# One decode-attention kernel: heads gathered in one PSUM bank per side, normalized once, and wo rows sent whole through four column groups

## The chip, the cores and the metric

One Trainium2 chip, of which the kernel uses one core. The metric is the device time of one execution in microseconds (us); where several runs are shown, their median. Times inside an execution are counted from the start of its profiled span.

## What is computed

Two attention layers of one token, A and B, each with 32 heads of 128, a K and a V cache of 16,384 positions, and bf16 data. A reads its whole caches, B only the last 4,096 positions. Both results, 512 numbers each, are written side by side.

```python
# A (B the same, with k and v cut to their last W = 4096 positions)
q = (x @ wq).reshape(B, Sq, Hq, Dh)                 # x: 1 x 512, wq: 512 x 4096
scores = einsum("bhqd,bhkd->bhqk", q, k) * (Dh ** -0.5)
p = softmax(scores)
o = einsum("bhqk,bhkd->bhqd", p, v)
out_A = o.reshape(B, Sq, Hq * Dh) @ wo              # wo: 4096 x 512
out = concatenate([out_A, out_B], axis=-1)          # 1 x 1 x 1024
```

## The kernel before

**Tiles.** The work is cut into 20 tiles of 8 MB of K and 8 MB of V. A tile of side A holds two heads (`a_pair`): a head's positions lie on 64 partitions, 256 on each. A tile of side B holds two units of four heads (`b_window`), each head on 32 partitions with 128 positions on each. `steps` puts B's four tiles at places 0, 7, 13 and 19, so the last tile is one of B's, with two units.

**Scores on VectorE.** For each half of a tile, `scores_prod` (L202) multiplies K in place with q, spread over the partitions; `scores_tree` (L208, L212) adds the 128 products pairwise and reduces the last eight. `tile_max` (L220, L224) and `max_all` (L230, L234, L237) find the maximum of each head, by a transpose on TensorE, and bring it back to one number per partition; L237 is an f32 matmul with an identity.

**Softmax and V.** `soft` on ScalarE takes the exponentials with their sums per partition (L251, sums in `un.cs`) and multiplies them by a mask for each head (L258), so that one matmul serves all heads of a unit. `soft_sum` (L266) adds the sums of a head's partitions on TensorE, `recip` (L274) inverts them on VectorE. `pv` (L283) runs 64 (A) or 32 (one unit of B) matmuls of 512 columns: four positions at once, into four groups of PSUM rows (column groups of 32), which TensorE works on at the same time. Each head then has 4 x 4 partial results, in a bank of 128 x 512. L290 copies the bank out with the factor 1/sum, four f32 matmuls (L294) with slices of `fold` pick and add the right pieces, and L299 writes the heads' columns into `s.O` (128 x 32).

**The output projection.** `permute_o` (L303 to L312) turns `s.O` into the order in which wo's rows lie on the partitions (row 32p + r on partition p, `load_wo`), giving `s.Op`. `project_out` (L319) sends each of the 32 rows r through four column groups, 128 output columns to each: 128 matmuls of 128 columns per side, all 32 weight columns being copies of one column of `s.Op`. L329 or L332 casts, and one DMA per side stores four partitions of 128 numbers.

**Order and buffers.** The order is the one of the source (`manual_schedule`). Each engine works through its own instructions in that order; all loads are issued by SyncE (SP), x and A's store by ScalarE. K has two slots (`kring`), V one (`vring`); wo takes V's slot after the last but one `pv`, and the last V goes into a K slot. In step T, VectorE does tile T's scores, while the softmax and `pv` of tile T-1 run on the other engines. wo of A comes as one load of 4 MB, that of B in pieces of 16, 8, 4, 3 and 1 rows. After the last tile: `permute_o(A)`, maxima, softmax, sums, two `pv`, `permute_o(B)`, projections of A and of B.

The names that the prediction uses: `sm` (PSUM tile of maxima and sums), `o` (PSUM banks of `pv`), `oc`, `oT`, `op`, `OA`/`OB`, `OpA`/`OpB`, `out_rows`, `wot` (wo in memory), `vlast` (the last V).

Of the kernel before, what the change touches and what calls it, by code (L numbers as in the profile page):

```python
# [25 lines left out]
def kernel(  # L26
# [30 lines left out]
    ps_s = ctx.enter_context(tc.tile_pool(name="ps_s", bufs=2, space=bass.MemoryType.PSUM))  # L57
# [13 lines left out]
    ident = singles.tile([P, P], BF16, tag="ident")  # L71
    one_b = singles.tile([1, 1], BF16, tag="one_b")
    pick = singles.tile([HQ, P + 4], BF16, tag="pick")
    fold = singles.tile([P, QR], F32, tag="fold")

    A, B = _Side(), _Side()
    for k, (s, n, x, wq, wo, nh) in enumerate(((A, "A", A_x, A_wq, A_wo, 2), (B, "B", B_x, B_wq, B_wo, 4))):
        s.n, s.k, s.x, s.wq, s.wo, s.nh = n, k, x, wq, wo, nh
        s.units = 1 if s is A else 2
        s.xT = singles.tile([P, KC], BF16, tag=f"xT{n}", name=f"xT{n}")  # L80
        s.q = singles.tile([P, HQ // nh, DH], BF16, tag=f"q{n}", name=f"q{n}")
        s.O = singles.tile([P, HQ], BF16, tag=f"O{n}", name=f"O{n}")
        s.Op = singles.tile([P, HQ], BF16, tag=f"Op{n}", name=f"Op{n}")
        s.mask = singles.tile([P, nh], F32, tag=f"mask{n}", name=f"mask{n}")
        s.rows = singles.tile([P, P], F32, tag=f"rows{n}", name=f"rows{n}")
# [59 lines left out]
    def make_masks(s):  # L145
        nc.vector.tensor_reduce(out=s.mask[:, :], in_=by_head(s, identf[:, :]), axis=AX.X, op=ALU.add)
        G = P // (4 * s.nh)
        nc.vector.tensor_copy(
            s.rows[:, :].rearrange("p (g h c) -> p g h c", g=G, h=s.nh),
            s.mask[:, :].unsqueeze(1).unsqueeze(3).broadcast_to([P, G, s.nh, 4]),  # L150
        )

    def turn_x(s, xrow):
        ps = ps_t.tile([P, KC], F32, tag="tp", name="xps")
        xr = xrow[:, s.k, :].rearrange("o (p c) -> o c p", c=KC)
        for c in range(KC):
            nc.tensor.matmul(ps[:, c : c + 1], lhsT=xr[:, c, :], rhs=one_b[:, :], start=True, stop=True)
        nc.vector.tensor_copy(s.xT[:, :], ps[:, :])
# [57 lines left out]
    def tile_max(T):  # L216
        un = tiles[T]
        U = un.s.units
        m = small.tile([P, 2], F32, tag="m", name="m")
        nc.vector.tensor_reduce(  # L220
            out=m[:, 0:U], in_=un.sc[:, :].rearrange("p (u n) -> p u n", u=U), axis=AX.X, op=ALU.max
        )
        un.sm = ps_m.tile([P, 512], F32, tag="sm", name="sm")
        nc.tensor.transpose(un.sm[0:U, 0:P], m[:, 0:U], identf[:, :])  # L224

    def max_all(T):
        un = tiles[T]
        s, U = un.s, un.s.units
        M = small.tile([2, 4], F32, tag="M", name="M")
        nc.vector.tensor_reduce(  # L230
            out=M[0:U, 0 : s.nh], in_=by_head(s, un.sm[0:U, 0:P]), axis=AX.X, op=ALU.max
        )
        Mr = one.tile([2, P], F32, tag="Mr", name="Mr")
        nc.vector.tensor_copy(  # L234
            by_head(s, Mr[0:U, :]), M[0:U, 0 : s.nh].unsqueeze(2).broadcast_to([U, s.nh, P // s.nh])
        )
        nc.tensor.matmul(  # L237
            un.sm[:, 128 : 128 + U], lhsT=Mr[0:U, :], rhs=identf[0:U, 0:U], start=True, stop=True
        )

    def soft(T):
        un = tiles[T]
        s, U = un.s, un.s.units
        bias = small.tile([P, 2], F32, tag="bias", name="bias")
        nc.scalar.activation(out=bias[:, 0:U], in_=un.sm[:, 128 : 128 + U], func=ACT.Copy, scale=-inv)  # L245
        p = one.tile([P, 2 * CH], BF16, tag="p", name="p")
        un.cs = small.tile([P, 2], F32, tag="cs", name="cs")
        pm = one.tile([P, 8 * CH], BF16, tag="pm", name="pm")
        un.pm = []
        for u in range(U):  # L250
            nc.scalar.activation(  # L251
                out=un.part(p, u), in_=un.part(un.sc, u), func=ACT.Exp, scale=inv, bias=bias[:, u : u + 1],
                accum_out=un.cs[:, u : u + 1],
            )
            n = un.n * s.nh
            un.pm.append(pm[:, u * n : (u + 1) * n].rearrange("p (i h c) -> p i h c", h=s.nh, c=4))
            for j in range(s.nh):
                nc.scalar.activation(  # L258
                    out=un.pm[u][:, :, j, :], in_=un.part(p, u).rearrange("p (i c) -> p i c", c=4),
                    func=ACT.Copy, scale=s.mask[:, j : j + 1],  # L260
                )

    def soft_sum(T):
        un = tiles[T]
        U = un.s.units
        nc.tensor.matmul(  # L266
            un.sm[:, 136 : 136 + U], lhsT=un.s.rows[:, :], rhs=un.cs[:, 0:U], start=True, stop=True
        )

    def recip(T):  # L270
        un = tiles[T]
        U = un.s.units
        un.r = small.tile([P, 2], F32, tag="r", name="r")
        nc.vector.reciprocal(un.r[:, 0:U], un.sm[:, 136 : 136 + U])  # L274

    def pv(T, u):
# [13 lines left out]
        nc.scalar.activation(out=osb[:, :], in_=o[:, :], func=ACT.Copy, scale=un.r[:, u : u + 1])  # L290
        oc = ps_s.tile([P, 4], F32, tag="sp", name="oc")
        sel = fold[:, 0:rows].rearrange("k (h c) -> k c h", c=4)
        for j in range(4):
            nc.tensor.matmul(  # L294
                oc[:, 0 : s.nh], lhsT=osb[:, j * P : (j + 1) * P], rhs=sel[:, j, :],
                start=(j == 0), stop=(j == 3),
            )
        col = s.nh * (s.units * un.g + u)
        nc.scalar.copy(s.O[:, col : col + s.nh], oc[:, 0 : s.nh])  # L299

    def permute_o(s):
        oT = ps_t.tile([HQ, P], BF16, tag="tp", name="oT")
        nc.tensor.transpose(oT[:, :], s.O[:, :], ident[:, :])  # L303
        oTs = one.tile([HQ, P], BF16, tag="oTs", name="oTs")
        nc.scalar.copy(oTs[:, :], oT[:, :])
        op = ps_t.tile([P, HQ], F32, tag="tp", name="op")
        for j in range(4):
            nc.tensor.matmul(
                op[:, :], lhsT=pick[:, 4 - j : 4 - j + P], rhs=oTs[:, j * HQ : (j + 1) * HQ],
                start=(j == 0), stop=(j == 3),  # L310
            )
        nc.scalar.copy(s.Op[:, :], op[:, :])  # L312

    def project_out(s):
        w = DN // NG
        ps = ps_s.tile([P, w], F32, tag="sp", name="out_rows")
        for r in range(HQ):
            for g in range(NG):
                nc.tensor.matmul(  # L319
                    ps[QR * g : QR * (g + 1), :],  # L320
                    lhsT=s.Op[:, r : r + 1].broadcast_to([P, QR]),
                    rhs=s.wo_t[:, r, g * w : (g + 1) * w],
                    start=(r == 0), stop=(r == HQ - 1),
                )
        rows = one.tile([P, w], BF16, tag=f"rows_out{s.n}", name="rows_out")
        dst = out[0, 0, s.k * DN : (s.k + 1) * DN].rearrange("(g f) -> g f", g=NG)
        src = rows[:, :].rearrange("(g x) f -> g x f", g=NG)[:, 0, :]
        if s is A:
            nc.scalar.copy(rows[:, :], ps[:, :])  # L329
            nc.scalar.dma_start(out=dst, in_=src)  # L330
        else:
            nc.vector.tensor_copy(rows[:, :], ps[:, :])  # L332
            nc.sync.dma_start(out=dst, in_=src)

    wo_pieces = (16, 8, 4, 3, 1)
    with tc.manual_schedule():
        xrow = one.tile([1, 2, D], BF16, tag="pm", name="xrow")
        for s in (B, A):
            nc.scalar.dma_start(out=xrow[:, s.k, :], in_=s.x[0, :, :])
# [10 lines left out]
        nc.vector.memset(one_b[:, :], 1.0)  # L350
        nc.vector.tensor_copy(ident[:, :], identf[:, :])
        clear_x(B, flat(scratch[:, :, :]))
        clear_x(A, one.tile([P, 2 * KC * P], BF16, tag="o4", name="xbA")[:, :])
        zeros = flat(scratch[:, :, :])[:, 0 : 512]
        for o in o_banks:
            nc.tensor.matmul(o[:, :], lhsT=zeros[:, 0:P], rhs=zeros, start=True, stop=True)
        for s in (B, A):
            make_masks(s)
        nc.vector.tensor_reduce(
            out=fold[:, :], in_=identf[:, :].rearrange("p (g x) -> p x g", g=NG), axis=AX.X, op=ALU.add  # L360
        )
        nc.vector.memset(pick[:, :], 0.0)
        nc.vector.tensor_copy(
            pick[:, 4 : 4 + P].rearrange("h (m k) -> h m k", k=4)[:, :, 0], identf[0:HQ, 0:HQ]
        )
        for s in (B, A):
            turn_x(s, xrow)
# [5 lines left out]
        for T in range(NT):  # L373
# [7 lines left out]
            if T >= 1:  # L381
                max_all(T - 1)
                soft(T - 1)
                soft_sum(T - 1)
            scores_tree(T, 0)
            if T >= 1:
                recip(T - 1)
# [13 lines left out]
        permute_o(A)  # L401
        max_all(NT - 1)
        soft(NT - 1)
        soft_sum(NT - 1)
        recip(NT - 1)
        for u in range(2):
            pv(NT - 1, u)
        permute_o(B)
        project_out(A)
        project_out(B)  # L410
# [30 lines left out]
```

## Time and profile before

| | us |
|---|---|
| time, median of 3 runs (826.05 to 826.29) | 826.10 |
| time of the profiled execution | 825.77 |
| its span in the profile | 824.0 |
| VectorE (DVE) busy | 760.8 (92%) |
| TensorE matmuls (PE) busy | 203.3 (25%) |
| ScalarE (ACT) busy | 67.6 (8%) |
| mean granted TensorE clock | 0.584 of full |
| read from HBM | 352.32 MB, 428 GB/s over the span |

A group of the profile reads: line, engine, operation, tile written <- tiles read, shapes, count, then busy us and mean ns of one instruction, then the engine's idle time ahead of them and what ended it. PE is a matmul, PEld a weight load, SPq and ACTq are the parts of an engine that issue DMAs. An f32 matmul that is no transpose shows as two records. In the chain of waits "issue" is time for which the profile names no cause. The granted clock is the share of TensorE's full clock in a stretch; it takes the values 0.5 and 1.0, and other values are means.

### The profile page before, as it was taken

How to read it: one execution, taken by the hardware profiler on the slowest of the kernel's cores; microseconds unless marked ns; L12 is line 12 of the kernel's file. 1: busy time of each engine (PE TensorE's matmuls, PEld its weight loads, DVE VectorE, ACT ScalarE, POOL GpSimd, SP SyncE). 2: the span in 40 equal slices, each digit the busy share in tenths (PEclk: the TensorE clock that was granted, in tenths of full speed). 3: DMA queues.
4: the chain of work that ended last, by engine and by line, in shares of the span. 5: the costliest groups of instructions: out<-in, count | busy, mean ns of one | idle time of the engine just before them, and what ended most of it. 6: DMA issues, size and time to landing. Idle time of an engine off the chain costs nothing.

```text
span 824.0 us, 4577 instructions
## 1 busy us (share of the span) xinstructions
PE 203.3 (25%) x1912; PEld 101.1 (12%) x1912; DVE 760.8 (92%) x340; ACT 67.6 (8%) x192; POOL 0.7 (0%) x6
## 2 busy tenths in 40 slices
PE   4402212303030203230312213030503030303126
PEld 1101100101010101120101101010201010101014
DVE  2899999999999999999999999999999999999980
ACT  0102000001010000100000000010200000000011
POOL 0000000000000000000000000000000000000000
PEclk9765555565565655555655565555555565555567
DMA  9999999999999999999999999999999999999996
GB/s 383 434 439 427 452 433 431 439 426 437 426 439 429 421 442 443 414 452 423 440 426 440 426 439 416 447 426 423 440 442 424 445 427 439 424 425 441 421 433 282
DMA packets 8104, 352.61 MB, mean 428 GB/s; under 512 B 914, under 2 KB 1044, under 8 KB 1300
## 3 DMA queue, kind: packets, MB, share of 16 engines
q1 hardware_dynamic: 8072, 352.33, 99.1%
q8 instruction: 14, 0.23, 0.1%
q14 instruction: 6, 0.05, 0.0%
q10 hardware_dynamic: 12, 0.00, 0.0%
HBM read 352.32 MB, written 0.00 MB: 428 GB/s over the span
## 4 chain that ended last, share of the span: by engine, by line
DMA 48%; DVE 48%; PE 2%; issue 1%; ACT 1%; SPq 0%; DVEq 0%; ACTq 0%
DMA kt<-in_A_k_cache_dram 44%; DVE kt L202 22%; DVE kt L208 22%; DMA kt<-in_B_k_cache_dram 5%; DVE sc L212 3%; PE out_rows L319 1%; PE o L283 1%; DVE Mr L234 0%; PE oc L294 0%; DVE M L230 0%; ACT o L290 0%; ACT pm L258 0%; SPq L134 0%; ACT p L251 0%; DVE m L220 0%
## 5 line engine op out<-in xcount | busy, mean ns | idle before, releaser
L208 DVE TENSOR_TENSOR kt<-kt 128x8192 bf16<-128x8192 bf16 (+3 forms) x160 | 344.9, 2156 | 4.8
L202 DVE TENSOR_TENSOR kt<-kt,qA 128x16384 bf16<-128x16384 bf16 x32 | 277.8, 8682 | 11.4 <-DMA kt<-in_A_k_cache_dram 11.4
L283 PE MATMUL o<-vt,pm 128*8 128x512 bf16 (+1 forms) x1216 | 112.8, 549 | 132.9 <-DMA vt<-in_A_v_cache_dram 132.9
L202 DVE TENSOR_TENSOR kt<-kt,qB 128x16384 bf16<-128x16384 bf16 x8 | 69.4, 8681 | 14.4 <-DMA kt<-in_B_k_cache_dram 14.4
L224 PE MATMUL sm<-identf,m 128*1 128x128 f32 (+1 forms) x20 | 7.4, 372 | 231.6 <-DVE m L220 231.6
L283 PEld LDWEIGHTS <-pm 128*8 128x8 bf16 (+1 forms) x1280 | 38.9, 113 | 199.1 <-issue 183.8
L237 PE MATMUL sm<-identf,Mr 1*128 1x1 f32 (+1 forms) x40 | 11.6, 357 | 176.1 <-DVE Mr L234 176.1
L212 DVE TENSOR_REDUCE sc<-kt 128x128 f32<-128x1024 bf16 x40 | 48.8, 1220 | 2.7
L290 ACT ACTIVATE o<-o,r 128x512 f32<-128x512 f32 x24 | 16.5, 687 | 252.6 <-PE o L283 235.5
L245 ACT ACTIVATE bias<-sm 128x1 f32<-128x1 f32 (+1 forms) x20 | 3.4, 171 | 411.4 <-PE sm L237 411.4
L294 PE MATMUL oc<-fold,o 128*128 128x2 f32 (+1 forms) x192 | 29.4, 275 | 28.0 <-ACT o L290 28.0
L294 PEld LDWEIGHTS oc<-fold,o 128*128 128x128 f32 x192 | 27.3, 219 | 42.7 <-ACT o L290 42.7
L237 PEld LDWEIGHTS sm<-identf,Mr 1*128 1x128 f32 (+1 forms) x40 | 9.9, 305 | 182.2 <-DVE Mr L234 182.2
L224 PEld LDWEIGHTS sm<-identf,m 128*1 128x1 f32 (+1 forms) x20 | 1.6, 79 | 233.1 <-issue 222.1
L332 DVE CAST rows_out<-out_rows 128x128 bf16<-128x128 f32 x1 | 0.3, 291 | 16.9 <-PE out_rows L319 16.9
L258 ACT ACTIVATE pm<-p,maskA 128x256 bf16<-128x256 bf16 x32 | 14.5, 501 | 0.5
L266 PE MATMUL sm<-cs,rowsA 128*128 128x1 f32 x32 | 9.4, 362 | 14.3 <-ACT p L251 14.3
L180 PE MATMUL qp<-wqt,xbA 128*128 128x512 bf16 x32 | 9.0, 452 | 10.9 <-DMA wqt<-in_A_wq_dram 10.9
L251 ACT ACTIVATE p<-sc,bias 128x256 bf16<-128x256 f32 (+1 forms) x24 | 11.3, 470 | 0.6
L258 ACT ACTIVATE pm<-p,maskB 128x128 bf16<-128x128 bf16 x32 | 10.2, 390 | 0.3
L266 PEld LDWEIGHTS sm<-cs,rowsA 128*128 128x128 f32 x32 | 8.0, 310 | 15.7 <-ACT p L251 15.7
L180 PE MATMUL qp<-wqt,scratch 128*128 128x512 bf16 x32 | 8.5, 431 | 4.8 <-DMA wqt<-in_B_wq_dram 4.8
(54 smaller groups left out, 73.3 us busy)
## 6 DMA issues: line engine op xcount, KB each, us to landing
kt<-in_B_k_cache_dram SPq DMA_DIRECT2D x8, 4096.0 KB, 39.4
vt<-in_B_v_cache_dram SPq DMA_DIRECT2D x6, 4096.0 KB, 28.1
vlast<-in_B_v_cache_dram SPq DMA_DIRECT2D x2, 4096.0 KB
wqt<-in_B_wq_dram SPq DMA_DIRECT2D x1, 4096.0 KB, 12.2
wqt<-in_A_wq_dram SPq DMA_DIRECT2D x1, 4096.0 KB, 30.5
wot<-in_A_wo_dram SPq DMA_DIRECT2D x1, 4096.0 KB, 24.0
wot<-in_B_wo_dram SPq DMA_DIRECT2D x1, 2048.0 KB, 28.5
wot<-in_B_wo_dram SPq DMA_DIRECT2D x1, 1024.0 KB, 30.5
```

Of the source, the lines that this page charges most:

```text
L180: nc.tensor.matmul(qp[:, :, :], lhsT=s.xb[:, j, c, :], rhs=wq[:, c, j, g : g + 4, :], start=(k == 0), stop=(k == n - 1),)
L202: nc.vector.tensor_tensor(out=k, in0=k, in1=s.q[:, j : j + 1, :].broadcast_to([P, CH, DH]), op=ALU.mult)
L208: nc.vector.tensor_tensor(out=k[:, :, 0:w], in0=k[:, :, 0:w], in1=k[:, :, w : 2 * w], op=ALU.add)
L212: nc.vector.tensor_reduce(out=tiles[T].sc[:, u * CH : (u + 1) * CH], in_=k[:, :, 0:8], axis=AX.X, op=ALU.add)
L224: nc.tensor.transpose(un.sm[0:U, 0:P], m[:, 0:U], identf[:, :])
L237: nc.tensor.matmul(un.sm[:, 128 : 128 + U], lhsT=Mr[0:U, :], rhs=identf[0:U, 0:U], start=True, stop=True)
L251: nc.scalar.activation(out=un.part(p, u), in_=un.part(un.sc, u), func=ACT.Exp, scale=inv, bias=bias[:, u : u + 1], accum_out=un.cs[:, u : ...
L258: nc.scalar.activation(out=un.pm[u][:, :, j, :], in_=un.part(p, u).rearrange("p (i c) -> p i c", c=4), func=ACT.Copy, scale=s.mask[:, j : ...
L266: nc.tensor.matmul(un.sm[:, 136 : 136 + U], lhsT=un.s.rows[:, :], rhs=un.cs[:, 0:U], start=True, stop=True)
L283: nc.tensor.matmul(o[r0 : r0 + rows, :], lhsT=un.pm[u][:, i, :, :].rearrange("p a b -> p (a b)"), rhs=V[T][:, u * un.n + 4 * i : u * un.n ...
L290: nc.scalar.activation(out=osb[:, :], in_=o[:, :], func=ACT.Copy, scale=un.r[:, u : u + 1])
L294: nc.tensor.matmul(oc[:, 0 : s.nh], lhsT=osb[:, j * P : (j + 1) * P], rhs=sel[:, j, :], start=(j == 0), stop=(j == 3),)
```

## The change

- `pv` copies its bank without a factor (L278 of the changed file) and adds its pieces by one f32 matmul of 512 columns with a shifted `s.fold` into a bank of its side, `s.acc`, where each head has four rows of its own. `soft_sum`, `recip`, the four small matmuls and `s.O` go. The sums stay in `s.cs` until the end.
- `gather_o`, once for each side: the sums of all heads by one matmul, their reciprocals, and from the bank of the side the block that belongs to each row, by a product with `quad` and a strided reduction on VectorE.
- `spread_o`, for both sides at once: one f32 matmul with `fours`, then for each side a product with the reciprocals and a strided reduction into `s.Op`. It replaces `permute_o`.
- `project_rows`: each row of wo goes whole, 512 columns, through one of four column groups (32 matmuls instead of 128); ScalarE and VectorE copy a half each. A's four groups are added by one f32 matmul, and its row is stored by four DMAs of ScalarE. For B this is done with 28 rows; four f32 matmuls in column groups add them, and the last four rows follow as before. B's store is cut into two, on ScalarE's and SyncE's queues.
- The pieces of B's wo are 16, 8, 4, 2, 2 rows. L237 is a transpose now. The two x's are turned together, by one set of matmuls with two columns. The banks of `pv` are cleared by VectorE. Constants are made at the start accordingly.

The diff, cut to its core:

```diff
-        nc.tensor.matmul(
-            un.sm[:, 128 : 128 + U], lhsT=Mr[0:U, :], rhs=identf[0:U, 0:U], start=True, stop=True
-        )
+        nc.tensor.transpose(un.sm[:, P : P + U], Mr[0:U, :], identf[0:U, 0:U])
...
-        un.cs = small.tile([P, 2], F32, tag="cs", name="cs")
+        col = s.units * un.g
-                accum_out=un.cs[:, u : u + 1],
+                accum_out=s.cs[:, col + u : col + u + 1],
...
@@ -287,56 +275,111 @@
                 start=(i < NG), stop=(i >= n - NG),
             )
         osb = one.tile([P, 512], F32, tag="o4", name="o4")
-        nc.scalar.activation(out=osb[:, :], in_=o[:, :], func=ACT.Copy, scale=un.r[:, u : u + 1])
-        oc = ps_s.tile([P, 4], F32, tag="sp", name="oc")
-        sel = fold[:, 0:rows].rearrange("k (h c) -> k c h", c=4)
-        for j in range(4):
+        nc.scalar.copy(osb[:, :], o[:, :])
+        per = QR // rows
+        q, off = divmod(s.units * un.g + u, per)
+        nc.tensor.matmul(
+            s.acc[QR * q : QR * (q + 1), :], lhsT=s.fold[:, (per - 1 - off) * rows : (per - 1 - off) * rows + QR],
+            rhs=osb[:, :], start=(off == 0), stop=(off == per - 1),
+        )
+
+    def square():
+        return one.tile([P, P], F32, tag="sq", name="sq")
+
+    def gather_o(s, both):
+        n = HQ // s.nh
+        sums = square()
+        nc.vector.tensor_tensor(
+            out=sums[:, :].rearrange("p (t h c) -> p t h c", t=n, h=s.nh),
+            in0=s.cs[:, :].unsqueeze(2).unsqueeze(3).broadcast_to([P, n, s.nh, 4]),
+            in1=s.mask[:, :].unsqueeze(1).unsqueeze(3).broadcast_to([P, n, s.nh, 4]), op=ALU.mult,
+        )
+        s.ps = ps_t.tile([P, 1], F32, tag="tp", name="sums")
+        nc.tensor.matmul(s.ps[:, :], lhsT=sums[:, :], rhs=ones[:, :], start=True, stop=True)
+        s.rq = small.tile([P, 5], F32, tag="rq", name="rq")
+        nc.vector.reciprocal(s.rq[:, 4:5], s.ps[:, :])
+        nc.vector.tensor_scalar(
+            out=s.rq[:, 0:4], in0=quad[:, :], scalar1=s.rq[:, 4:5], scalar2=None, op0=ALU.mult
+        )
+        own = one.tile([P, 512], F32, tag="o4", name="own")
+        nc.vector.tensor_tensor(
+            out=own[:, :].rearrange("p (c d) -> p c d", c=4), in0=s.acc[:, :].rearrange("p (c d) -> p c d", c=4),
+            in1=quad[:, :].unsqueeze(2).broadcast_to([P, 4, DH]), op=ALU.mult,
+        )
+        nc.vector.tensor_reduce(
+            out=both[:, s.k, :], in_=own[:, :].rearrange("p (c d) -> p d c", c=4), axis=AX.X, op=ALU.add
+        )
+
+    def spread_o(both):
+        ps = ps_t.tile([P, 2, P], F32, tag="tp", name="heads")
+        nc.tensor.matmul(ps[:, :, :], lhsT=fours[:, :], rhs=both[:, :, :], start=True, stop=True)
+        for s in (B, A):
+            d = square()
+            nc.vector.tensor_tensor(
+                out=d[:, :].rearrange("p (j r) -> p j r", j=4), in0=ps[:, s.k, :].rearrange("p (j r) -> p j r", j=4),
+                in1=s.rq[:, 0:4].unsqueeze(2).broadcast_to([P, 4, HQ]), op=ALU.mult,
+            )
+            with nc.allow_low_precision("attention output in the dtype of the reference"):
+                nc.vector.tensor_reduce(
+                    out=s.Op[:, :], in_=d[:, :].rearrange("p (j r) -> p r j", j=4), axis=AX.X, op=ALU.add
+                )
+
+    def o_column(s, r):
+        return s.Op[:, r : r + 1].broadcast_to([P, QR])
+
+    def project_rows(s, n):
+        ps = ps_t.tile([P, DN], F32, tag="tp", name="wide")
+        for r in range(n):
+            g = r % NG
             nc.tensor.matmul(
-                oc[:, 0 : s.nh], lhsT=osb[:, j * P : (j + 1) * P], rhs=sel[:, j, :],
-                start=(j == 0), stop=(j == 3),
+                ps[QR * g : QR * (g + 1), :], lhsT=o_column(s, r), rhs=s.wo_t[:, r, :],
+                start=(r < NG), stop=(r >= n - NG),
             )
-        col = s.nh * (s.units * un.g + u)
...
+        wide = one.tile([P, DN], F32, tag="o4", name="wide_sb")
+        h = DN // 2
+        nc.scalar.copy(wide[:, 0:h], ps[:, 0:h])
+        nc.vector.tensor_copy(wide[:, h:DN], ps[:, h:DN])
+        return wide
+
+    first = A.fold[:, QR - A.rows : QR - A.rows + 1]
+
+    def project_a():
+        wide = project_rows(A, HQ)
+        ps = ps_m.tile([1, DN], F32, tag="sm", name="out_a")
+        nc.tensor.matmul(ps[:, :], lhsT=first, rhs=wide[:, :], start=True, stop=True)
+        row = one.tile([1, DN], BF16, tag="p", name="row_a")
+        nc.scalar.copy(row[:, :], ps[:, :])
+        for f in range(0, DN, DN // 4):
+            nc.scalar.dma_start(out=out[0, :, f : f + DN // 4], in_=row[:, f : f + DN // 4])
+
+    def project_b():
+        w = DN // NG
+        n = HQ - 4
+        wide = project_rows(B, n)
+        ps = ps_m.tile([P, w], F32, tag="sm", name="out_b")
+        for g in range(NG):
             nc.tensor.matmul(
-                op[:, :], lhsT=pick[:, 4 - j : 4 - j + P], rhs=oTs[:, j * HQ : (j + 1) * HQ],
-                start=(j == 0), stop=(j == 3),
+                ps[QR * g : QR * (g + 1), :], lhsT=first.broadcast_to([P, QR]), rhs=wide[:, g * w : (g + 1) * w],
+                start=True, stop=False,
             )
-        nc.scalar.copy(s.Op[:, :], op[:, :])
-
-    def project_out(s):
-        w = DN // NG
-        ps = ps_s.tile([P, w], F32, tag="sp", name="out_rows")
-        for r in range(HQ):
+        for r in range(n, HQ):
             for g in range(NG):
                 nc.tensor.matmul(
-                    ps[QR * g : QR * (g + 1), :],
-                    lhsT=s.Op[:, r : r + 1].broadcast_to([P, QR]),
-                    rhs=s.wo_t[:, r, g * w : (g + 1) * w],
-                    start=(r == 0), stop=(r == HQ - 1),
+                    ps[QR * g : QR * (g + 1), :], lhsT=o_column(B, r), rhs=B.wo_t[:, r, g * w : (g + 1) * w],
+                    start=False, stop=(r == HQ - 1),
                 )
-        rows = one.tile([P, w], BF16, tag=f"rows_out{s.n}", name="rows_out")
-        dst = out[0, 0, s.k * DN : (s.k + 1) * DN].rearrange("(g f) -> g f", g=NG)
+        rows = one.tile([P, w], BF16, tag="rows_b", name="rows_b")
+        nc.vector.tensor_copy(rows[:, :], ps[:, :])
+        dst = out[0, 0, DN : 2 * DN].rearrange("(g f) -> g f", g=NG)
         src = rows[:, :].rearrange("(g x) f -> g x f", g=NG)[:, 0, :]
-        if s is A:
...
+        for queue, g in ((nc.scalar, 0), (nc.sync, 2)):
+            queue.dma_start(out=dst[g : g + 2, :], in_=src[g : g + 2, :])
+
+    wo_pieces = (16, 8, 4, 2, 2)
     with tc.manual_schedule():
-        xrow = one.tile([1, 2, D], BF16, tag="pm", name="xrow")
+        xrow = one.tile([2, D], BF16, tag="pm", name="xrow")
         for s in (B, A):
-            nc.scalar.dma_start(out=xrow[:, s.k, :], in_=s.x[0, :, :])
+            nc.scalar.dma_start(out=xrow[s.k : s.k + 1, :], in_=s.x[0, :, :])
         scratch = kslot("scratch")
         new_k(0)
         wqt = vslot("wqt")
...
@@ -381,10 +426,8 @@
             if T >= 1:
                 max_all(T - 1)
                 soft(T - 1)
-                soft_sum(T - 1)
             scores_tree(T, 0)
             if T >= 1:
-                recip(T - 1)
                 for u in range(tiles[T - 1].s.units):
                     pv(T - 1, u)
             if T + 1 < NT:
@@ -398,16 +441,16 @@
             scores_prod(T, 1)
             scores_tree(T, 1)
             tile_max(T)
-        permute_o(A)
         max_all(NT - 1)
         soft(NT - 1)
-        soft_sum(NT - 1)
-        recip(NT - 1)
+        both = one.tile([P, 2, P], F32, tag="sc", name="both")
+        gather_o(A, both)
         for u in range(2):
             pv(NT - 1, u)
-        permute_o(B)
-        project_out(A)
-        project_out(B)
+        gather_o(B, both)
+        spread_o(both)
+        project_a()
+        project_b()
 
 
 # ---- launch: one core; inputs and outputs as the reference has them ----
```

## The prediction

> **What bounds the kernel now.** First the page: which resource is full from end to end. Its columns are a queue's packets, MB and share of 16 DMA engines.
>
> ```profile
> span 824.0 us, 4577 instructions
> ...
> DMA  9999999999999999999999999999999999999996
> ...
> q1 hardware_dynamic: 8072, 352.33, 99.1%
> ```
>
> Reads fill the span; nothing here changes a byte of them, so only the edge after the last landing can move. The chain of waits shows it (start, length, what):
>
> ```profile
> 803.18 0.58 PE sm L266 x2
> 803.77 3.55 PE o L283 x32
> ...
> 813.95 4.86 PE out_rows L319 x221
> 818.80 1.39 issue
> 820.19 0.71 PE out_rows L319 x35
> 820.89 0.02 issue
> 820.92 0.29 DVE rows_out L332
> ```
>
> TensorE catches up with the projection, stands still for 1.39 us, and does 35 matmuls after the reads have ended. Stretches of the tail (last columns: granted clock, DMA share, GB/s):
>
> ```profile
> 814.69:818.11 3.42, 3.42 (x144) 3.42 (x136) 0.00 (x0) 0.27 (x1) 0.00 (x0) 0.50 0.79 312
> 818.11:821.52 3.41, 1.37 (x80) 1.02 (x68) 0.29 (x1) 0.00 (x0) 0.00 (x0) 1.00 0.14 53
> ```
>
> So work and DMA end almost together: B's pieces of wo land at 815.0, 817.5, 818.7, 819.8 and, the last row, 820.07 (the trace's semaphore updates). A tail that is slower by more than a few tenths takes over the end. [...]
>
> Durations for the sum, from the timeline and the groups by form:
>
> ```profile
> 803.70 3.59 PE L283 MATMUL o<-vlast,pm 128*16 128x512 bf16 x32
> ...
> 809.06 1.90 PE L283 MATMUL o<-vlast,pm 128*16 128x512 bf16 x32
> ```
> ```profile
> L224 PE MATMUL sm<-identf,m 128*1 128x128 f32 x16 | 6.0, 372 | 179.8 <-DVE m L220 179.8
> ...
> L303 PE MATMUL oT<-ident,OA 128*32 128x128 bf16 x1 | 0.3, 289 | 0.0
> ...
> L359 DVE TENSOR_REDUCE fold<-identf 128x32 f32<-128x128 f32 x1 | 0.4, 360 | 0.0
> ```
>
> The same 32 matmuls through four column groups take 3.59 us at half clock and 1.90 at full.
>
> **Start: nothing.** New constants, folds and two bank clears replace the old ones: about +1.1 us on DVE (clears 0.49 each by L162's 128x512 row, reductions 0.25 to 0.36). DVE now waits until 7.95 for A's x anyway, and the turned x's (0.3) with their spreading (0.74+0.49) end near 9.5; the first projection waits for wq until 12.93. Without this cover it would cost up to 1.1.
>
> **Each tile: nothing.** L266 (0.58), eight L294 records (1.05) and L299 (0.16) go; one f32 fold of 512 columns (two records) comes. TensorE then idles about 8 us for V. The V slot comes free while K is still in flight: at 204.56, K landing at 217.5, 13 us of cover. The reciprocal leaves DVE (0.07 each), which waits 0.5 us for K per tile anyway; only the last two count, -0.14.
>
> **Up to the last pair of folds: ahead by 1.2.** L237 becomes a transpose of one record instead of two: -0.21. The sums matmul L266 stood between the first mask pass (ready at 802.74) and L283 (803.70): -0.96. So the last tile's first 32 matmuls start at 803.70-0.14-0.21-0.96 = 802.4, end at 806.0 (3.59), the copy (0.69 and handoffs 0.1) at 806.8.
> The fold of 512 f32 columns is not in the trace. Two records of at least a bf16 row's 0.427 us per 512 columns at half clock give 0.85; twice that 1.71. L224 against L303, the same 128 columns, gives 84 ns per 128 columns more for f32: (0.427+4x0.084)x2 = 1.5 at half, 0.76 at full clock; I take that. [...] It begins at half clock and ends at full: about 1.3, end 808.1. Second half: 1.9, copy 0.8, fold 0.76 and 0.2 until read: 811.7, against 812.89 now.
>
> **New serial steps: 3.9 against 1.06.** Before, OB to Op (812.89 to 813.95) took 1.06 by ACT and TensorE. Now in a row: sums matmul 0.25 (two records 0.11 apart at full clock), reciprocal 0.16, scaling 0.12, product of 512 out of PSUM 0.65 (ACT's copy of that shape 0.69), strided reduction of 512 to 128 at 0.85 (0.68 by L220's slope, 1.0 by L359's), heads matmul of 256 f32 columns 0.6, and two times a product (0.25) and a strided reduction (0.36). Together 3.85 to 3.9: 815.6. Here the change falls 1.7 us behind. Bounds 3.0 to 4.6.
>
> **Projection.** 32 matmuls of 512 columns replace 128 of 128. TensorE has been nearly idle for 3.9 us, so they run at half clock: 3.6 (bounds 1.9 and 3.6): 819.2. Halves copied by ACT and DVE 0.5: 819.7. A's fold of 512 f32 columns, 0.76 to 1.5: on the present grid the clock rises only at 821.52: 821.2. B's 28 matmuls, mostly at full clock, 1.7 (to 3.2): 822.9.
> B's halves need ACT, and ACT has work ahead of that copy: A's row (0.58 by L184, 128x512) and four DMA issues. ACT's issues take 0.22 (second x row) to 0.61 (L330); I take the one-row one, with 0.05 between: 1.1. ACT is free at 822.95: just hidden. At 0.61 it costs 1.5 more. Then the copy 0.5, four f32 folds in column groups and 16 matmuls 0.7 (35 took 0.71; 0.5 to 1.2), DVE's cast 0.33: 824.6, against 821.21 now: **+3.4**.
> Pieces 2+2 instead of 3+1: same bytes (packets of 3 KB take 124 ns, of 1 KB 46: 170 for both splits). The instruction order shows the last piece now behind the landing of B's first 16 rows (its semaphore), 815.0; engines are still busy with older pieces then, and the rows are needed only near 824: nothing. Two stores of two partitions instead of one of four: the issue now takes 0.66; -0.3 to +0.2, taken 0.
>
> **Sum.** The profiled execution took 825.77 us (span 824.0 and 1.8 around it): 825.77+3.4 = 829.2. It lies 0.33 below the median of the runs, 826.1; for the median I say **829.5**.
>
> **Rivals.**
> 1. *TensorE is early and the last landing decides, not slower.* The 1.39 us pause has no semaphore in the trace that ends with it: the 4-row piece landed at 818.74, and the first instruction to resume, at 820.19, is a weight load that waits for nothing. A 16 KB instruction packet ran from 817.67 to 818.71, after 256 pairs in 5 us. With 32+28 wide matmuls the pause goes. [...] If all else is ready at 820.1, then eight matmuls (0.3) and the cast: store 0.45 earlier, 825.7 for the median. It decides if the steps from 811.7 to B's last copy fit in 8.4 us instead of the 11.7 I sum: rows and fold of A at full clock (-2.4) and 0.9 off DVE. [...] 0.12.
> 2. *Half way*: DVE steps at their low bound (-0.9) and the clock rising before A's fold (-0.75 and some): +1.3, 827.4, within 0.2%. [...] 0.13.
> 3. *ACT's stores stand ahead of B's copy*: 0.61 each, +1.5: 831.0. For it: both stores now take 0.61 and 0.66. 0.15.
> 4. *The reads end earlier or later*, by where fewer instruction packets fall: 16 engines finish between 816.3 and 819.6, so up to 2 us earlier if the late ones gain, and TensorE keeps up: below 824.4. 0.02.
>
> My forecast has 0.58 (own range 828.0 to 831.0). About 0.2% is what a measurement of this kernel can tell from no change, 1.65 us; the line lies at 827.75. Slower: forecast, rival 3, less a tail of the forecast: 0.72. Same: rivals 1 and 2 and that tail: 0.26. Faster: 0.02. The range 826.2 to 831.4 takes in rival 2 and the bounds of the unknown rows, and leaves rivals 1 and 4 and some of 3 out.
>
> **What would show it.** Right: after the last landing of wo (near 820.1) TensorE still works on A's rows or fold; their 32 matmuls take over 3 us; the chain runs through gather_o and spread_o on DVE for 3 to 4 us between the last fold and the first wide matmul. Step by step: last tile's L271 starts near 802.4; a fold spans 0.75 to 1.7; no pause without a wait in the projection. Wrong: wide matmuls at full clock, or B's 16 last matmuls begin right at the landing.

## The result and the profile after

The changed kernel took **830.86 us** (median of 4 executions, 830.70 to 832.67); the kernel before took 826.08 on the same chip (4 executions, 825.90 to 826.29). The ratio is 1.0063, with a 95% interval of 1.0045 to 1.008: slower by 4.8 us, more than the 1.65 us that this measurement can tell. In later jobs the kernel before had executions near 826.3, others near 828.5 and a few between, so the ratios below belong to their own job, and a comparison in microseconds takes the group near 826.3.

The profiled execution took 830.83 us with a span of 829.0, against 825.77 and 824.0. All but 0.3 of the 5.0 us arises behind the last tile's maximum (`m`), which begins at 798.82 instead of 798.50; in the profiled executions of both kernels and their variants it begins between 798.50 and 799.00. These are pieces of the chain that ended last, of the changed kernel (start, us, engine, tile, line). A fold is one of the new f32 matmuls that add up pieces; `accB` L281 is the last of those of `pv`:

```profile
810.88 1.05 PE accB L281 x2
811.93 0.33 PE sums L298 x2
...
812.28 0.18 DVE rq L300
...
812.48 0.23 DVE rq L301
812.71 0.60 DVE own L305
...
813.34 1.03 DVE both L309
...
814.41 1.13 PE heads L315 x2
...
817.04 3.63 PE wide L334 x32
...
820.74 0.38 ACT wide_sb L340
...
821.14 0.44 DVE wide_sb L341
...
822.68 0.58 ACT row_a L351
...
824.14 0.26 ACTq L353
...
824.50 0.38 ACT wide_sb L340
...
824.90 0.44 DVE wide_sb L341
...
826.05 0.29 DVE rows_b L372
```

Nothing in this stretch waits for a transfer. wo's last row lands at 820.30 (820.07 before), and the cast that ended 1.1 us behind it (821.21) now ends 6.0 us behind it (826.34). From 811.93 to 817.04 ten operations of PE and DVE stand in a row. Then come A's 32 wide matmuls, two copies, A's fold, A's row copy, ACT's four DMA issues and B's two copies, each waiting for the one before. The time between the end of one and the start of the next, mostly 0.02 to 0.04, is called a handoff below.

In the traces of both kernels the granted clock changes only at the bounds of a grid of 3.41 us: each of the 240 whole stretches of the kernel before and the 242 of the changed kernel lies at 0.5 or at 1.0. Stretches of the changed kernel (busy us and number of PE, PEld, DVE, ACT, POOL; then granted clock, DMA share, GB/s):

```profile
804.32:807.73 3.41, 2.72 (x27) 0.76 (x23) 0.10 (x1) 0.70 (x2) 0.00 (x0) 0.50 0.98 418
...
811.14:814.56 3.42, 1.25 (x5) 0.45 (x4) 2.01 (x4) 0.00 (x0) 0.00 (x0) 1.00 0.94 394
814.56:817.97 3.41, 1.90 (x14) 0.66 (x18) 1.32 (x4) 0.00 (x0) 0.00 (x0) 0.50 0.88 345
817.97:821.38 3.41, 2.68 (x28) 0.71 (x20) 0.23 (x1) 0.37 (x1) 0.00 (x0) 0.50 0.16 62
```

While DVE does the new steps (811.14 to 814.56), TensorE is busy for 1.25 us of 3.42. The two stretches after that run at half clock, and they hold all of A's wide matmuls.

### The profile page after: what moved, and what is told of

Same layout as the page of the kernel before. It is cut to its first block, busy times and chain, and to the rows that moved or that the text cites. A ratio compares the mean times of both kernels' runs of the same rounds, so it can differ in the third digit from the quotient of the medians.

```text
span 829.0 us, 3772 instructions
## 1 busy us (share of the span) xinstructions
PE 184.3 (22%) x1528; PEld 58.7 (7%) x1528; DVE 766.8 (92%) x340; ACT 61.5 (7%) x166; POOL 0.7 (0%) x6
## 4 chain that ended last, share of the span: by engine, by line
DMA 48%; DVE 48%; PE 2%; issue 1%; ACT 1%; SPq 0%; ACTq 0%; DVEq 0%
DMA kt<-in_A_k_cache_dram 43%; DVE kt L205 22%; DVE kt L211 22%; DMA kt<-in_B_k_cache_dram 5%; DVE sc L215 3%; PE o L271 1%; PE wide L334 0%; DVE Mr L237 0%; DVE M L233 0%; PE accB L281 0%; ACT pm L259 0%; ACT o L278 0%; PE heads L315 0%; DVE both L309 0%; ACTq L353 0%
## 5 line engine op out<-in xcount | busy, mean ns | idle before, releaser
L240 PE MATMUL sm<-identf,Mr 1*128 1x1 f32 (+1 forms) x20 | 5.2, 262 | 178.4 <-DVE Mr L237 178.4
L278 ACT COPY o<-o 128x512 f32<-128x512 f32 x24 | 14.0, 585 | 258.8 <-PE o L271 258.8
L281 PE MATMUL accA<-o,foldA 128*32 128x512 f32 x32 | 16.7, 605 | 11.1 <-ACT o L278 11.1
L240 PEld LDWEIGHTS sm<-identf,Mr 1*128 1x128 f32 (+1 forms) x20 | 3.5, 177 | 184.8 <-DVE Mr L237 184.8
L281 PE MATMUL accB<-o,foldB 128*32 128x512 f32 x16 | 10.4, 738 | 5.7 <-ACT o L278 5.7
L223 DVE TENSOR_REDUCE m<-sc 128x1 f32<-128x256 f32 (+1 forms) x20 | 8.4, 420 | 0.7
```

The lines of the kernel that those rows point to most:

```text
L223: nc.vector.tensor_reduce(out=m[:, 0:U], in_=un.sc[:, :].rearrange("p (u n) -> p u n", u=U), axis=AX.X, op=ALU.max)
L240: nc.tensor.transpose(un.sm[:, P : P + U], Mr[0:U, :], identf[0:U, 0:U])
L278: nc.scalar.copy(osb[:, :], o[:, :])
L281: nc.tensor.matmul(s.acc[QR * q : QR * (q + 1), :], lhsT=s.fold[:, (per - 1 - off) * rows : (per - 1 - off) * rows + QR], rhs=osb[:, :], s ...
```

## The experiments

The theory: the gather puts a serial chain across engines where TensorE worked before; the chain is paid in itself, and a second time by the clock that falls during it. The rivals: the copies and stores between the wide matmuls and the end cost the time; or the projection itself does.

**1. One engine per bank (`a_one_copy`).** The changed kernel, with A's bank copied whole by ScalarE and B's whole by VectorE:

```diff
-        nc.scalar.copy(wide[:, 0:h], ps[:, 0:h])
-        nc.vector.tensor_copy(wide[:, h:DN], ps[:, h:DN])
+        if s is A:
+            nc.scalar.copy(wide[:, :], ps[:, :])
+        else:
+            nc.vector.tensor_copy(wide[:, :], ps[:, :])
```

> The changed kernel, but each bank of wide rows is copied by one engine: A's whole by ScalarE, B's whole by VectorE. Theory (every step behind the last fold counts one for one, because the reads have ended at 820.3 and TensorE, ScalarE and VectorE hand on to each other): in the changed kernel the two halves of one bank do not overlap (0.38, then 0.44 after it); one copy of 512 takes about 0.59 (L278), so A's step is 0.27 shorter; B's copy no longer stands behind A's stores in ScalarE's queue and starts when B's matmuls end, near 823.9, and takes about 0.65: the cast begins 0.8 earlier, 830.0 us. Rival (the tail's length is hidden by something that ends later, or the halves did overlap in effect): 830.7 to 831.1.

Measured: 830.56 (median of 6, 830.35 to 830.74; ratio to the kernel before 1.0043, 1.0031 to 1.0056). Its chain:

```profile
820.61 0.59 ACT wide_sb L340
...
822.10 1.71 PE wide L334 x16
...
823.90 0.70 DVE wide_sb L342
```

One copy of 512 columns takes 0.59 on ACT, against 0.38 and 0.44 one behind the other. B's copy starts as soon as B's wide matmuls end (823.81) and no longer behind ACT's issues; the cast ends at 825.63, 0.7 earlier, of which 0.14 was there when the wide matmuls began (816.90). The median gained 0.3, under the 0.8 that was expected. A part of the difference lies outside the profiled span: these executions take 1.9 to 2.1 us beyond their span, the first ones of the changed kernel 1.8. By the spans (828.4 to 828.7, against 828.9 to 829.1 and one of 830.9) the gain is 0.5. The direction was right, and the size lies between 0.3 and 0.7.

**2. The gather alone (`a_old_projection`)**, the changed kernel with the projection of the kernel before:

```diff
...
-        project_a()
-        project_b()
+        project_out(A)
+        project_out(B)
```

> The changed kernel with the projection of before (256 matmuls of 128 columns, no folds, one store per side), the new gathering kept. Theory: the projection's share of the 5.1 us is what its steps cost, 9.3 us from the first wide matmul to the cast's end. The old projection from 817.04 takes 5.6 us of matmuls, or 6.9 if TensorE again pauses for its instructions: cast's end at 823.0 to 824.3 instead of 826.34, so 827.5 to 828.8 us. Rival (the gathering alone is to blame, and the wide projection is as fast as the old one): 830.5 or more.

Measured: 827.34 (827.09 to 828.39, 10 executions), 0.16 under the lower expected bound and 1.0 above the group near 826.3; the ratio of 1.0001 (0.999 to 1.0012) doesn't tell it from no change. Its cast ends at 822.46, 1.25 later than in the kernel before.

**3. The projection alone (`b_new_projection`)**, the kernel before with the new `project_a`, `project_b` and pieces of wo.

> The kernel before with the new projection and pieces of 16, 8, 4, 2, 2 rows, the old gathering kept (A's row lies in another buffer). Theory: Op is ready at 813.95, the new projection takes 9.3 us from there, a little less if the clock is still full at its start: cast's end near 823.0 instead of 821.2, so 827.5 to 828.1 us. Rival (the gathering alone is to blame): 825.7 to 826.1. Rival (the wide rows alone, at half clock, are to blame for all): 830 or more.

Measured: 827.67 (median of 10, 827.33 to 833.15), inside the expected band and 1.4 above that group; ratio 1.0023 (1.0006 to 1.0039). Its wide matmuls start at 813.96, take 3.54, and the cast ends at 823.19, 2.0 later.

So alone the parts cost up to 1.0 and 1.4 (1.25 and 2.0 by the cast's end), together 4.8 (5.1). A likely reason stands in the profile of the kernel before: TensorE has done all but 35 of the projection's 256 pairs of weight load and matmul by 818.80 and then pauses for 1.39 us, so the first microsecond or two of a later tail may be paid from that slack, and the second part finds none left. The pause is not all of it, since 0.73 of it still stands in the chain of experiment 2; and the lost clock is no effect of both parts together, since the wide matmuls ran at half clock in experiment 3 too. How the difference divides stays open.

**4. TensorE kept busy (`a_busy`)**, the changed kernel with extra matmuls of 512 columns into a bank that nobody reads, 11 behind B's sums matmul and 6 behind the heads matmul:

```diff
+    def keep_busy(n):
+        for _ in range(n):
+            nc.tensor.matmul(
+                o_banks[0][:, :], lhsT=A.q[:, 0, :], rhs=A.q[:, 0:4, :], start=True, stop=True
+            )
...
+        if s is B:
+            keep_busy(11)
...
+        keep_busy(6)
```

> The changed kernel with 17 extra matmuls of 512 columns whose result nobody reads, 11 behind B's sums and 6 behind the heads matmul, in the time that TensorE waits for VectorE. Theory (the wide matmuls and the heads matmul run at half clock because TensorE was idle for 4 us before): the granted clock stays full, the heads matmul spans 0.65 instead of 1.13, A's 32 matmuls 1.9 instead of 3.6: 2.1 us less, 828.7 us. Rival (the wide matmuls are slow for another reason, weights or PSUM): their span stays 3.6 and the time 830.5 to 831.5.

Measured: 828.71 (828.37 to 829.43, 10 executions; ratio 1.002, 1.001 to 1.003), 2.1 under the changed kernel. Its timeline:

```profile
817.24 1.91 PE L343 MATMUL wide<-wot,OpA 128*32 128x512 bf16 x32 [0.23 <-DVE OpA L332]
```

The same 32 matmuls take 1.9 instead of 3.6. They start 0.2 later: the clock rose at 808.75 here and not at 807.73, which put the last fold 0.6 later, and the extra matmuls held the heads matmul back by another 0.2, while that matmul then took 0.51 instead of 1.13. The cast ends 1.5 earlier in this execution, the slowest of the ten (829.43). The clock is thus 1.5 (profiled executions) to 2.1 (medians) of the 4.8 us.

**5. All three mends (`a_all`)**: extra matmuls (9 and 5), one engine per bank, and A's four stores issued by SyncE.

> The changed kernel with its tail mended at three places: 9 and 5 extra matmuls that nobody reads keep the clock up, each bank of wide rows is copied by one engine, and A's four stores are issued by SyncE. Theory (terms behind the last fold add up): 2.1 us for the clock, 0.3 to 0.8 for the copies and the queue, 0.3 less delay of the heads matmul than with 11 and 6 extra ones: 827.5 to 828.0 us, still above the kernel before, because gathering and spreading alone put the projection's start 2 to 3 us later. Rival (something else than these terms makes the tail long): 828.7 or more.

Measured: 828.33 (828.04 to 828.92, 10 executions; ratio 1.0014, 1.0003 to 1.0025). That is 0.3 above the upper expected bound: the mends of the copies and issues, with the fewer extra matmuls, gained 0.4 on experiment 4. By the spans (medians 826.3 and 826.9) it is 0.6, since these executions take 2.0 us beyond their span and those of experiment 4 1.8. What remains is 2.0 above the group near 826.3; the new serial steps are still all there (`OpA` is ready at 816.84).

**6. Only the front edits (`b_order`)**, the kernel before with L237 as a transpose and the last tile's sums behind the first 32 matmuls:

```diff
...
+        if T == NT - 1 and u == 0:
+            soft_sum(T)
+            recip(T)
...
-        soft_sum(NT - 1)
-        recip(NT - 1)
```

> The kernel before with two small edits taken over from what the change does well: L237 as a transpose (one record instead of two), and in the last tile the sums matmul and the reciprocal behind the first 32 matmuls of the last V instead of ahead of them. Theory: these 32 matmuls start 1.2 us earlier (802.5), the whole tail with them, TensorE's pause ends before the last landing of wo, and the end is set by that landing (820.1) plus the last matmuls, cast and store: 0.4 to 0.5 us below the kernel before, 825.6 beside 826.1. Rival (the pause is a wait for the last landing itself, so nothing moves): the time of the kernel before within 0.1.

This one failed. Measured: 828.18 (median of 12) in two groups, 5 executions from 826.10 to 826.28 and 7 from 828.12 to 828.34; ratio 0.9999 (0.9986 to 1.0012). One of the second group was profiled; its chain:

```profile
809.89 3.55 PE o L281 x31
...
817.29 5.41 PE out_rows L320 x241
822.70 0.32 issue
823.02 0.43 PE out_rows L320 x15
```

The second 32 matmuls, which took 1.90 in the kernel before, take 3.55 here: the granted clock stays at 0.50 until 821.25. A start 0.8 earlier (802.93) bought nothing here, because the clock did not rise. The profile also bears on the pause, beside which the prediction set an instruction packet, and which the author read as a wait for instructions: it ends at 823.02, 2.8 us after the last landing of wo (820.21) and 1.43 after a 16 KB instruction packet ended (821.59).

**7. The pause moved (`b_shift`)**: 48 small matmuls at the start of the kernel before, so 96 more instructions of TensorE, with their weight loads, ahead of the tail.

> [...] Theory (the 1.39 us pause in the projection is a wait for instructions): the pause comes 48 pairs earlier, after about 173 of the 256 pairs, near 817.5, begins where no wait for wo stands, and ends about 1.4 us after a 16 KB instruction packet has ended, not at a landing of wo; time 825.6 to 826.3. Rival (it is a wait for pieces of wo): the pause stays behind pair 221 and ends at the landing of the last piece.

Measured, one execution: 828.51, no pause at all, and the projection in one piece of 5.91 us (817.73 to 823.64), at half clock until 822.30. A 16 KB instruction packet ended at 820.53; the matmul expected to wait came at 822.23, 1.7 later, by when the pauses of the other runs (which ended 1.34 to 1.48 behind a packet) were over. It fits the reading but doesn't test it: inconclusive.

**8 and 9. The front edits with TensorE kept busy**: `b_busy` adds 4 extra matmuls behind the last tile's additions and 4 behind L237; `b_busy_more` adds 28: 16 between the last tile's additions, 7 behind L237, 5 while ScalarE copies the banks.

> The kernel before with the two edits of b_order and eight extra matmuls of 512 columns that nobody reads: four behind the last additions of the last tile (near 797.3) and four behind L237 (near 800.5), so that TensorE is busy from there and the clock rises before or in the last tile's first 32 matmuls. Theory (the kernel before has two tails, one of 826.0 with the clock risen at about 807.9, one of 828.5 where it stays at half until 821): the high group goes away, the first 32 matmuls take 1.9 to 3.0 instead of 3.6, and all executions lie at 825.5 to 826.2, against 826.0 or 828.5 before. Rival (the two groups have another cause, such as the memory): the high group stays, at 828 or more in a third of the executions.

> The kernel before with the two edits of b_order and 28 extra matmuls that nobody reads, so that TensorE has work from 793 on wherever it would wait in the tail: 16 during the last additions on VectorE, 7 behind L237, 2 and 3 while ScalarE copies the two banks of the last tile. Theory (before's tail is long enough to show only because of the half clock and the pause for instructions): the clock rises before 800 and stays up, both halves of the last V take about 1.9, the projection and its pause are over before 820, and the end is the last landing of wo plus 0.7 for four matmuls and the cast: 825.2 to 825.8 in all executions. Rival (the extra matmuls cost as much as they bring, by late weight loads or late sums): 826 to 827.5, as the run with eight of them.

Measured: `b_busy` 826.79 (median of 12, 825.60 to 827.33; ratio 0.9996, 0.9986 to 1.0006). The group above 828 is gone, but the median was above the expected band. That excess lies outside the span: the spans are 823.6 to 824.3, where the expected band less the usual 1.8 gives 823.7 to 824.4, but these executions take 1.9 to 3.0 us beyond them. No run shows what that time is. The first 32 matmuls took 3.05, just above the expected 3.0. `b_busy_more`: **825.46** (median of 11, 825.17 to 825.64; ratio 0.9975, 0.9967 to 0.9984), the fastest here, under every execution of the kernels before and after. Its timeline:

```profile
802.73 1.90 PE L289 MATMUL o<-vlast,pm 128*16 128x512 bf16 x32 [0.48 <-ACT pm L264]
...
815.25 1.08 PE L330 MATMUL out_rows<-wot,OpB 128*32 128x128 bf16 x64 [1.56 <-DMA wot<-in_B_wo_dram]
...
820.00 0.62 PE L330 MATMUL out_rows<-wot,OpB 128*32 128x128 bf16 x16 [0.40 <-DMA wot<-in_B_wo_dram]
```

Both halves of the last V run at full clock, TensorE waits for each piece of wo, and the cast ends at 820.96, 0.7 behind the last landing (820.26). Here the last bytes decide, and a shorter tail would bring no more.

**10. The changed kernel again (`a_again`)**, unmodified.

> The changed kernel itself, for its spread beside that of the kernel before on the same chip. Theory (its tail too depends on where the clock's grid lies): executions at 830.4 to 831.0 and some near 832.7, none below 829.5. Rival (one value, the 832.7 of the first runs was an accident): all within 830.5 to 831.1.

Measured: 830.56, 830.57, 830.67, 830.76 and 832.30 (ratio 1.0039, 1.0024 to 1.0054; that job's kernel before, 826.07 to 828.72, has 6 of 15 executions above 828). The one of 832.30 was profiled. Up to the start of A's fold it agrees with the chain shown above to about 0.2 us; behind it:

```profile
823.26 2.69 PE wide L334 x12
```

The clock stays at half until 825.24, and the cast ends 1.5 later. So the changed kernel, too, has a slower kind of execution; in the profiled one the clock rose 3.9 us later (825.24 against 821.38).

## Why the prediction was right, and where it was not

The sign, the forecast and the mechanism held: 829.5 was predicted with 826.2 to 831.4, 830.86 was measured. Of the profiled times, +3.4 was forecast and +5.1 came. Step by step:

- **Start, tiles, store pieces: nothing.** Held, but for the 0.3 by which the last tile came later, which is within the spread of the executions. DVE's set-up ends at 5.98 and x arrives at 7.90; the first projection runs at 12.89.
- **Ahead by 1.2 up to the last folds.** Nearly held: the first 32 matmuls start at 802.79 (802.4 forecast), and the fold is read at 811.93 (811.7), 0.96 ahead of the kernel before. The working was wrong by one thing, and was lucky there: it put the fold of 512 f32 columns and the second 32 matmuls in a row. The timeline shows them start side by side (the fold is written into one column group):

```profile
807.08 0.92 PE L281 MATMUL accB<-o,foldB 128*32 128x512 f32 x1 [0.69 <-ACT o L278]
...
807.08 1.12 PE L271 MATMUL o<-vlast,pm 128*16 128x512 bf16 x9
```

  Side by side they still took 3.09 together (807.08 to 810.17), where the sum had 1.3 and 1.9, so the end came out right for another reason than the one given. At full clock the two records of the last fold take 1.05 in the chain, where 0.76 and 0.2 until it is read were taken.
- **New serial steps, 3.9.** This step was mis-sized: 5.1, above its upper bound of 4.6. Durations come to 4.86, handoffs to 0.25, which the sum did not hold. Of the difference, 0.53 is the heads matmul (1.13 against 0.6): the clock fell at 814.56, while it ran; with the clock kept up it took 0.51 to 0.71 (experiments 2 and 4). The strided reduction of 512 to 128 took 1.03, as by the dearer of its two rows, where a value between them was chosen (0.85); the scaling 0.23 against 0.12.
- **A's wide matmuls at half clock, 3.6.** Held: 3.63, and experiment 4 shows that it is the clock (1.9 with TensorE kept busy). No run shows a rule by which idle time must halve the clock, or by which it can rise only at 821.52, as the sum had it for A's fold: it rose at 821.38 in the changed kernel and at 825.24 in `a_again`, and in the trace of the kernel before it rose behind stretches in which TensorE was busy for 2.65 to 3.42 us, but not behind one of 3.25 (353.90 to 357.31).
- **Halves copied in 0.5.** Mis-sized, twice in the chain: 0.38, then 0.44, 0.84 with the handoff. The price assumed that ACT and DVE copy at the same time. The program has VectorE's half wait for ScalarE's, which reads the other half of the same bank (in the trace it waits for ScalarE's semaphore). In this kernel two engines for the two halves of one bank were slower than ACT alone: experiment 1 has 0.59.
- **B's copy "just hidden" behind ACT's row and issues.** The row copy and issues cost what was said (0.58 and 1.11), but A's row came 1.5 later than forecast and B's matmuls only 1.3 later (done at 824.16, forecast 822.9). So ACT, whose copy starts at 824.50, was last by 0.3. That is the start of rival 3, at a fifth of its price: its issues of 0.61 did not come (0.23 to 0.26 each).
- **The folds and 16 matmuls, 0.7, and the cast, 0.33.** Held: 0.65 and 0.29.

Over the tail: +0.2 up to the fold's reading, +1.2 in the serial steps, +0.9 in the two pairs of halves with their handoffs; less 0.5 in A's fold, for which the clock rose at 821.38, and 0.1 at the end: +1.7, which is 5.1 less 3.4.

Rival 1 was right that the pause would go: the projection has none now. Its 256 pairs in 5 us are not in the trace, in which 185 matmuls and 189 weight loads start in the 5.9 us from the start of the 16 KB packet before (811.75) to the start of this one (817.67). The rival missed in that nothing else was ready. `b_busy_more` shows the end that it described, one set by the last landing, at 825.46 where rival 1 gave 825.7. Rival 2 had VectorE's steps at their low bound; they lay at the other end. Rival 4 had the reads end earlier; wo's last landing moved by 0.2.

**Still open.** What makes the clock rise. The stretch 804.32 to 807.73 of the changed kernel was busy for 2.72 us, and the clock rose; in `b_order`, 804.20 to 807.60 was busy for 2.84 and 807.60 to 811.00 for 2.98, and it did not rise. The kernel before rose behind 2.84. Busy time in the trace doesn't separate them (its matmul ends are modelled, and some records are missing). The matmuls of 512 columns alone come nearer. They fill 2.71 of the changed kernel's stretch and all 2.84 of the one of the kernel before, but less of the two in `b_order`, where the sums and the small f32 matmuls of the last tile take the rest (line L281 alone; PE's and PEld's busy us and number, then granted clock, DMA share, GB/s):

```profile
804.20:807.60 3.40, 2.32 (x24) 0.55 (x16) 0.50 0.95 410
807.60:811.00 3.40, 1.18 (x12) 0.40 (x16) 0.50 0.95 405
```

That fits the clock of `b_order`, but it is no rule: in the changed kernel 346.93 to 350.34 was busy for 2.72 too, and half clock followed. Open too: why `b_order`'s faster executions, up to 826.28, gain nothing on the kernel before.

## What to carry to other kernels

Behind the last transfer, count the steps that stand in a row across engines, with a handoff each, and not the instructions: 805 fewer instructions (3772 for 4577) cost 4.8 us here, since the many small ones had been hidden under a transfer and the few new ones are not. Price TensorE's work there by the clock it will have: here a stretch that left it idle for two thirds was followed by half clock, where A's wide matmuls took 3.6 us instead of 1.9, and matmuls that nobody reads were worth their place. Test edits together as well as alone: here the parts cost up to 1.0 and 1.4, and together 4.8.

## What the runs showed of the hardware beyond that

- Two profiled executions of the changed kernel differ by the clock: it rose at 821.38 in the one of 830.83 us and at 825.24 in the one of 832.30 (`a_again`). With TensorE kept busy through the tail (`b_busy_more`) all 11 executions lie within 0.5 us, while the kernel before in the same job spread from 826.07 to 828.72. The kernel before was not profiled in an execution above 828; over the later jobs its executions with spans of 826.5 to 827.0 had a mean granted clock of 0.574 to 0.583, those with spans of 823.8 to 824.5 one of 0.580 to 0.596. The stretches above show that the busy share that a trace gives doesn't tell behind which of them the clock rises: it rose behind 2.72 us in the changed kernel, and not behind 2.98 in `b_order`.
- The pause in the projection ends 1.34 to 1.48 us after a 16 KB instruction packet's end: 1.48 in the kernel before, 1.42 in `a_old_projection`, 1.43 in `b_order`, 1.34 in `b_busy`, in the last before wo's last landing and in `b_order` long after it. So wo's landing isn't what it waits for, and the first instruction behind it names no semaphore in any of the four. In the chain that ended last of `a_old_projection` the pause stands between two stretches of the projection:

```profile
815.93 4.17 PE out_rows L335 x167
820.11 0.73 issue
820.84 1.30 PE out_rows L335 x77
```

  Its place tells more. It stands behind pair 221, 241, 233 and 179 of the projection (the kernel before, `b_order`, `b_busy`, `a_old_projection`). Counted from the start of the program up to the pause's end, TensorE has done the same number of matmuls in the first three, and 256 fewer in the last (the number in brackets behind the first busy time, PE's; then PEld, DVE, ACT, POOL):

```profile
0.00:820.18 820.18, 202.60 (x1877) 100.58 (x1877) 760.46 (x339) 67.58 (x192) 0.70 (x6) 0.58 1.00 430
0.00:823.00 823.00, 197.53 (x1877) 95.64 (x1877) 760.47 (x339) 67.53 (x192) 0.70 (x6) 0.59 0.99 428
0.00:820.04 820.04, 202.07 (x1877) 96.14 (x1877) 760.49 (x339) 67.55 (x192) 0.70 (x6) 0.58 1.00 430
0.00:820.83 820.83, 181.80 (x1621) 60.25 (x1621) 765.67 (x337) 60.44 (x164) 0.70 (x6) 0.60 1.00 430
```

  `b_order` has 20 matmuls fewer ahead of the projection and `b_busy` 12 fewer, and the pause moved by 20 and 12 pairs. So in these four the pause belongs to a place in TensorE's instructions and ends 1.34 to 1.48 us behind an instruction packet. That it is a wait for instructions is the author's reading of this; no run shows it. `b_shift`, which was to move it on purpose, reaches the same count at 822.23, 1.7 us behind its packet, and has no pause.
- An f32 matmul into one column group of a bank ran beside bf16 matmuls into another bank: both started at 807.08 and took 0.92 and 1.12 us. Whether two engines can read two halves of one bank at once, no run here shows: the program made the second wait for the first.
